# Longer DMA estimates in the plan, a second buffer for turned keys, and operands at 512-byte starts, in a planned attention and feed-forward kernel on one Trainium2 core

## The chip, the core and the metric

The kernel runs on one core of a Trainium2 chip. Its engines are TensorE (PE in the rows; PEld is its weight load), VectorE (DVE), ScalarE (ACT), GpSimd (POOL) and SyncE (SP, which issues nearly all DMAs). The metric is device time in microseconds (us) of one execution; the median of three runs is given before the change. The profile is one more execution of the same program.

## What is computed

```python
for t in range(S):                                   # attention with a decaying state
    state = alpha[:, :, t, :, None] * state + einsum('bhd,bhe->bhde', k[:, :, t], v[:, :, t])
    y[:, :, t] = einsum('bhd,bhde->bhe', q[:, :, t], state)
x = y.transpose(0, 2, 1, 3).reshape(3072, 384)
x = ((x @ w_a) * (x @ w_b)) @ w_out                  # first layer, width 1536
h = x @ w_in                                         # second layer, width 2048
out = (maximum(h, 0) + alpha2 * minimum(h, 0)) @ w_out2
```

There are 4 batches, 8 heads, 768 steps and a head size of 48, all in float32. The first layer's weights come as float64.

## The kernel before

**Tiles and stages.** The 3,072 tokens are 24 chunks of 128 steps. Four chunks make a block of 512 tokens, so there are 6 blocks, numbered 0 to 5. The attention is done chunk by chunk and leaves each block as a tile `x` (a high and a low part in fp32r, which together hold the float32 value). The first layer takes `x` block by block in units of 256 columns of weights, and the second layer does the same once all its weights are rounded and stored in DRAM.

**Products.** Every product of the two layers is three products of parts: high by high, low by high, high by low. That is `mm3` (lines 926, 927 and 929): nine matmuls of 128 by 128 by 512 for one tile in PSUM. The intermediate value is split by ACT into `gh` and by DVE into `gl` (lines 950 and 954); `a_sb` (line 1057) is the product of the two branches of the first layer. The stationary operand of a matmul is a weight tile, the moving one is `x`, `gh` or `gl`.

**Attention of a chunk.** `ra` holds the decays and `kq` the keys and queries, both loaded by SP into two buffers each. DVE makes running products with two scans: `scan_r` (line 584) runs backwards with the constant `ones`, `recip` (line 590) puts reciprocals into the constant `invs`, `scan_a` (line 594) runs forwards with `invs`, and `mul` (line 599) scales `kq` with both. From block 2 on the keys are turned by DMA and not by PE: DVE transposes 32 by 32 squares into `kt` (line 660), four DMAs take them to DRAM (line 664, `ktd`) and four bring them back as `ks` (line 674). `kt` and `ks` share one buffer, so the transposition of a chunk waits until PE has used the `ks` of the chunk before it. PE then works in two steps: `pe_cross`, and `pe_own` (lines 786 and 793), which needs the half-way state that DVE adds up (`mid`, line 813) and which also computes the scores of the next chunk (line 625), so that it needs the next chunk's scaled `kq` too.

**The order.** Nothing is scheduled by the hardware's readiness alone: a planner in the kernel (class `Graph`) places every operation on its engine by a guessed duration, a guessed latency and a key (the time at which it is wanted), then tries 1,500 random changes of the keys of operations that begin in the first 120 us, and keeps the plan whose last PE operation ends first. Each engine then runs its instructions in that fixed order. A DMA has a duration on SP and a latency after it. Where the plan leaves PE idle at the start, `fill` puts matmuls without a use there (line 342).

**Memory.** Tiles lie in SBUF in the order of their pools: const, wpool (weights), pers (`ones`, `invs`, the states `Z`, `As`), xpool (`x`), cpool, gpool (`gh`, `gl`), tp (the attention's inputs). By the sizes, the weights begin at byte 2,752 of each partition, which is 192 past a multiple of 512; `x` begins at 136,960, `gh` at 186,112 and `gl` at 192,256, each 256 past a multiple of 512. All tiles of a kind have sizes that are multiples of 512 there, so every slice that a full-size matmul reads begins at the same distance.

Of the kernel before, what the change touches and what calls it, by code (L numbers as in the profile page):

```python
# [14 lines left out]
F32 = mybir.dt.float32  # L15
# [23 lines left out]
SPLIT = ((0, 0), (1, 0))  # L39
BY_BLOCKS = 2  # L40

ON_PE = (("a", 0), ("b", 0), ("o", 0))
# [11 lines left out]
SOON = 120000  # L54
SEED, TRIES, WORLDS = 2, 1500, 2

# [12 lines left out]
class Graph:  # L69
# [11 lines left out]
    def add(self, eng, dur, fn, key, deps=(), lat=0, after=(), pool=None, burst=False, line=None):  # L81
        o = Op()
        o.pool, o.hold, o.burst = pool, [], burst
        o.eng, o.dur, o.fn, o.key, o.lat = eng, dur - LEAD.get(eng, 0), fn, key, lat + LEAD.get(eng, 0)
        o.users, o.soft, o.n = [], [], len(self.ops)
        for d in {x.n: x for x in deps if x is not None}.values():
            d.users.append(o)
        for d in {x.n: x for x in after if x is not None}.values():
            d.soft.append(o)
        if line:  # L90
            if line in self.last and self.last[line] not in [x for x in after if x is not None]:
                self.last[line].soft.append(o)
            self.last[line] = o
        self.ops.append(o)
        return o
# [203 lines left out]
def body(tc, akq, v, vg, w_a, w_b, w_o1, w_in, w_o2, beta, out):  # L299
# [13 lines left out]
    with ExitStack() as ctx:  # L313
        ctx.enter_context(tc.manual_schedule())
        pool = lambda name, bufs=1, **k: ctx.enter_context(tc.tile_pool(name=name, bufs=bufs, **k))
        const, wpool, pers = pool("const"), pool("wpool"), pool("pers")
        xpool, cpool, gpool, tp = pool("xpool", 2), pool("cpool", 2), pool("gpool", 2), pool("tp", 2)
        dram = pool("dram", space=DRAM)
# [8 lines left out]
        betaT = const.tile([P, F2], F32, name="betaT")  # L327
        ones = pers.tile([P, NJ, CH + 1], F32, name="ones")
        invs = pers.tile([P, NJ, CH + 1], F32, name="invs")
        Z = pers.tile([P, BC, NJ, D], F32, name="Z")  # L330
        At = pers.tile([P, 2 * NC], F32, name="As")
        x2d = [dram.tile([P, 2, KT, MB], F32, name=f"x2d{n}") for n in range(NB)]
# [3 lines left out]

        warm = ones.bitcast(BF16)[:, 0, 2 : 2 + 2 * CH]

# [4 lines left out]

        nc.gpsimd.memset(ones, 0.0)
        nc.gpsimd.memset(ones[:, :, 0:1], 1.0)
        nc.gpsimd.memset(invs, 0.0)
        make_identity(nc, eye)
# [174 lines left out]
        xring, lring, rring, vring = Ring(2), Ring(2), Ring(2), Ring(2)  # L522
        aring, kring, sring = Ring(1), Ring(1), Ring(1)
        both = ps_att.tile([P, 2, 2 * NC // 2], F32, name="both")
# [4 lines left out]
        state = [[] for _ in range(BC)]  # L529
        sums = [At[:, NC + i * NJ * D : NC + (i + 1) * NJ * D].rearrange("p (j d) -> p j d", d=D) for i in range(2)]  # L530
        slots = [Z[:, c] for c in range(BC)] + sums[1:]

        def place(g):
            n, c = divmod(g, BC)
            key = c * 1000 - 100000 if n == 0 else block_at[n] - (BC - c) * 12000 - 14000
            if n == 1:
# [7 lines left out]
        def inputs(g):  # L544
# [38 lines left out]
            def scan_r():  # L583
                nc.vector.tensor_tensor_scan(
                    out=s["ra"][:, 0 : NA - 1][:, ::-1], data0=s["ra"][:, : NA - 1 : -1],
                    data1=ones.rearrange("p j t -> p (j t)"), initial=0.0, op0=ALU.mult, op1=ALU.add,
                )

            def recip():
                nc.vector.reciprocal(invs[:, :, 0:1], r0())  # L590

            def scan_a():
                a = s["ra"][:, NA - 1 : 2 * NA - 2]
                nc.vector.tensor_tensor_scan(out=a, data0=a, data1=invs.rearrange("p j t -> p (j t)"),
                                             initial=0.0, op0=ALU.mult, op1=ALU.add)
# [4 lines left out]

            turned = n >= BY_BLOCKS
            r = A("DVE", 1220, scan_r, [la])
            rc = A("DVE", 180, recip, [r, before["scan"]])
            sa = before["scan"] = A("DVE", 1220, scan_a, [rc])
            slack = SLACK if not start else 0
# [35 lines left out]
        def chunk(g):  # L641
# [16 lines left out]
            def turn():  # L658
                s["kt"] = tp.tile([P, NJ, P], F32, name="kt", tag="ks", bufs=1)
                nc.vector.transpose(s["kt"], kT())  # L660

            def away(b):
                def f():
                    nc.sync.dma_start(
                        ktd[g].rearrange("t j a f -> t (j a) f")[:, :, b * SQ : (b + 1) * SQ],
                        s["kt"][b * SQ : (b + 1) * SQ].rearrange("p j (a d) -> p (j a) d", d=SQ),
                    )
# [9 lines left out]
            if turned:  # L677
                x = A("DVE", 650, turn, [k1, *kring.take()])
                lhold.append(x)
                moved = [A("SP", 430, away(b), [x], 0, 2000) for b in range(BT)]  # L680
                x = None
                back_at = []
                for a in range(BT):
                    x = A("SP", 350, back(a), moved, 0, 3800, after=[x])
                    back_at.append(x)
# [564 lines left out]
```

## Time and profile before

| | |
|---|---|
| median of 3 runs | 943.03 us (941.46 to 948.37) |
| the profiled execution | 943.25 us |
| its span, first to last instruction | 941.5 us |
| PE busy | 932.5 us, 99% of the span |
| DVE busy | 564.0 us, 60% |
| ACT busy | 245.2 us, 26% |

The page of the profile gives the busy time of each engine, the same in 40 slices of the span, and the chain of waits. Other views used below are the table by stretches of time (busy time and granted clock in each), the instructions in order of time, the groups by line and shape, and the list of waits by engine. The busy time of a matmul in the rows is from its start to its modelled end, so matmuls that follow each other overlap there; the time that one costs is the distance between starts.

### The profile page before, as it was taken

The numbers are of one execution on the slowest core, as the hardware profiler recorded it, in microseconds if no ns is written. First come the engines' busy times: TensorE is split into PE (matmuls) and PEld (weight loads), VectorE is DVE, ScalarE is ACT, GpSimd is POOL, SyncE is SP. The second block draws the span as 40 slices with busy tenths as digits, with TensorE's granted clock in tenths as the row PEclk, the third lists the DMA queues.
The fourth block names the chain that finished last, engine by engine and source line by source line (L and its number), as shares of the span: only waits on it lengthen the run. The fifth ranks groups of instructions, "written<-read, shape, count | busy, mean of one in ns | idle before, by whom it ended". The sixth has DMA issues, their size and how long they took to land.

```text
span 941.5 us, 15646 instructions
## 1 busy us (share of the span) xinstructions
PE 932.5 (99%) x6637; PEld 760.1 (81%) x6637; DVE 564.0 (60%) x865; ACT 245.2 (26%) x406; POOL 2.2 (0%) x11
## 2 busy tenths in 40 slices
PE   9999999999999999999999999999999999999998
PEld 7788887888888788787888888888888888888886
DVE  8999964674886687663232264554545545545554
ACT  3555531223333333331122121111111111111111
POOL 0000000000000000000000000000000000000000
PEclk9999999999999999999999999999999999999999
DMA  9973103563657767763266620100200200200000
GB/s 353 403 262 102 32 1 79 159 189 137 210 162 228 249 207 217 241 175 93 82 235 202 212 91 1 68 34 1 89 12 1 101 1 0 101 1 1 34 0 34
DMA packets 75238, 112.89 MB, mean 120 GB/s; under 512 B 38689, under 2 KB 48417, under 8 KB 75169
## 3 DMA queue, kind: packets, MB, share of 16 engines
q1 hardware_dynamic: 75024, 111.77, 36.1%
q8 instruction: 52, 0.85, 0.4%
q14 instruction: 18, 0.14, 0.0%
q10 hardware_dynamic: 144, 0.13, 0.0%
HBM read 78.97 MB, written 30.93 MB: 117 GB/s over the span
## 4 chain that ended last, share of the span: by engine, by line
PE 90%; DVE 5%; DMA 2%; issue 1%; SPq 1%; ACT 0%; DVEq 0%; ACTq 0%
PE acc L926 12%; PE acc L929 12%; PE acc L927 12%; PE pi L926 7%; PE pi L927 7%; PE pi L929 7%; PE pb L926 5%; PE pa L926 5%; PE pb L927 5%; PE pa L929 5%; PE pa L927 5%; PE pb L929 5%; PE both L786 2%; PE both L625 1%; DMA v<-in_v 1%; DMA ra<-in_akq 1%
## 5 line engine op out<-in xcount | busy, mean ns | idle before, releaser
L950 ACT CAST gh<-ng 128x512 fp32r<-128x512 f32 x96 | 59.5, 620 | 329.8 <-DVE ng L1163 274.0
L1159 DVE TENSOR_SCALAR ng<-pi,betaT 128x512 f32<-128x512 f32 x96 | 72.1, 751 | 105.6 <-PE pi L929 104.7
L954 DVE TENSOR_TENSOR gl<-ng,gh 128x512 fp32r<-128x512 f32 x96 | 66.3, 690 | 79.6 <-ACT gh L950 79.6
L926 PE MATMUL pi<-x,v 128*128 128x512 f32 x288 | 113.3, 393 | 0.0
L929 PE MATMUL acc<-gl,v 128*128 128x512 f32 x288 | 113.1, 393 | 0.0
L926 PE MATMUL acc<-gh,v 128*128 128x512 f32 x288 | 112.9, 392 | 0.0
L927 PE MATMUL pi<-x,v 128*128 128x512 f32 x288 | 112.7, 391 | 0.0
L927 PE MATMUL acc<-gh,v 128*128 128x512 f32 x288 | 112.1, 389 | 0.0
L1057 DVE TENSOR_TENSOR a_sb<-a_sb,pb 128x512 f32<-128x512 f32 (+1 forms) x76 | 49.9, 656 | 83.3 <-PE pb L929 83.3
L926 PE MATMUL pb<-x,wb 128*128 128x512 f32 (+1 forms) x228 | 87.8, 388 | 0.6 <-DVE a_sb L1057 0.6
L926 PE MATMUL acc<-gh,wo 128*128 128x512 f32 (+1 forms) x228 | 88.4, 388 | 0.0
L926 PE MATMUL pa<-x,wa 128*128 128x512 f32 (+1 forms) x228 | 87.3, 386 | 0.0
L929 PE MATMUL acc<-gl,wo 128*128 128x512 f32 (+1 forms) x228 | 86.8, 381 | 0.0
L927 PE MATMUL pb<-x,wb 128*128 128x512 f32 (+1 forms) x228 | 86.0, 380 | 0.5 <-DVE wb L453 0.5
L927 PE MATMUL acc<-gh,wo 128*128 128x512 f32 (+1 forms) x228 | 86.4, 379 | 0.0
L927 PE MATMUL pa<-x,wa 128*128 128x512 f32 (+1 forms) x228 | 85.9, 380 | 0.0
L950 ACT CAST gh<-a_sb 128x512 fp32r<-128x512 f32 (+1 forms) x76 | 45.3, 596 | 140.8 <-DVE a_sb L1057 131.5
L929 PE MATMUL pi<-x,v 128*128 128x512 f32 x288 | 81.6, 391 | 0.0
L1054 ACT COPY a_sb<-pa 128x512 f32<-128x512 f32 (+1 forms) x76 | 42.7, 562 | 107.1 <-PE pa L929 106.9
L1163 DVE SCALAR_TENSOR_TENSOR ng<-pi,ng 128x512 f32<-128x512 f32 x96 | 66.3, 691 | 3.1
L926 PEld LDWEIGHTS pi<-x,v 128*128 128x128 f32 x288 | 54.1, 188 | 13.7 <-DVE ng L1163 2.1
L954 DVE TENSOR_TENSOR gl<-a_sb,gh 128x512 fp32r<-128x512 f32 (+1 forms) x76 | 50.1, 659 | 25.0 <-ACT gh L950 24.9
(126 smaller groups left out, 1360.3 us busy)
## 6 DMA issues: line engine op xcount, KB each, us to landing
kq<-in_akq SPq DMA_DIRECT2D x24, 512.0 KB, 5.1
w2d<-ws SPq DMA_DIRECT2D x16, 768.0 KB, 5.1
v<-w2d SPq DMA_DIRECT2D x16, 768.0 KB, 5.9
x2d<-x SPq DMA_DIRECT2D x18, 512.0 KB, 3.7
x<-x2d SPq DMA_DIRECT2D x6, 1536.0 KB, 6.9
ra<-in_akq SPq DMA_DIRECT2D x24, 258.5 KB, 3.9
v<-in_v SPq DMA_DIRECT2D x24, 256.0 KB, 5.0
rs<-in_w_in SPq DMA_DIRECT2D x8, 768.0 KB, 6.0
```

What stands on the lines that cost most here:

```text
L625: nc.tensor.matmul(a[hs, i, j, :], kT()[ps, j, hs], qT()[ps, j, hs], start=True, stop=True, skip_group_check=True)
L786: nc.tensor.matmul(y_of(k, half(p), part_of(h)), s["v"][part_of(h), 2 * j + i, :], s["As"][part_of(h), i, j, :], start=first, stop=False, ...
L926: nc.tensor.matmul(o, lh, rh, start=first and n == 0, stop=False)
L927: nc.tensor.matmul(o, ll, rh, start=False, stop=False)
L929: nc.tensor.matmul(o, lh, rl, start=False, stop=last and n == len(pairs) - 1)
L950: nc.scalar.copy(gq[idx][0], src())
L954: nc.vector.tensor_tensor(out=gl, in0=src(), in1=gh.bitcast(F32), op=ALU.subtract)
L1054: nc.scalar.copy(b["a"], ba["t"])
L1057: nc.vector.tensor_tensor(out=b["a"], in0=b["a"], in1=bb["t"], op=ALU.mult)
L1159: nc.vector.tensor_scalar(out=b["n"], in0=bh["t"], scalar1=0.0, scalar2=betaT[:, i : i + 1], op0=ALU.min, op1=ALU.mult)
L1163: nc.vector.scalar_tensor_tensor(out=b["n"], in0=bh["t"], scalar=0.0, in1=b["n"], op0=ALU.max, op1=ALU.add)
```

## The change

The plan's figures for DMAs grow: the four DMAs that take a turned chunk away count 640 ns on SP and 3,500 ns after it (430 and 2,000 before), the four that bring it back 640 and 5,000 (350 and 3,800). Every DMA of SP that is wanted later than 110 us in the plan counts 3,500 ns more (`SPARE`). The keys of blocks 2 to 5 are spaced 16,000 ns apart instead of 12,000 (`PACE`). The seed of the random search is another one. The turned keys `kt` get a place of their own at the end of `At`, apart from `ks`. The constants `ones` and `invs` become one tile `heads`: `recip` overwrites its four first columns, and GpSimd sets them to 1.0 again after `scan_a`, before the next `scan_r` may run. Last, a pad of 320 bytes stands ahead of the weights and `pers` moves to the end, so that the weights begin at byte 3,072, `x` at 125,952, `gh` at 175,104 and `gl` at 181,248, all multiples of 512.

```diff
+PACE = 16000
+STEADY, SPARE = 110000, 3500
+PAD = 80
-SEED, TRIES, WORLDS = 2, 1500, 2
+SEED, TRIES, WORLDS = 6, 1500, 2
+        lat += SPARE if eng == "SP" and key > STEADY else 0
-        const, wpool, pers = pool("const"), pool("wpool"), pool("pers")
-        xpool, cpool, gpool, tp = pool("xpool", 2), pool("cpool", 2), pool("gpool", 2), pool("tp", 2)
+        const, wpool, xpool = pool("const"), pool("wpool"), pool("xpool", 2)
+        cpool, gpool, tp, pers = pool("cpool", 2), pool("gpool", 2), pool("tp", 2), pool("pers")
-        ones = pers.tile([P, NJ, CH + 1], F32, name="ones")
-        invs = pers.tile([P, NJ, CH + 1], F32, name="invs")
+        const.tile([P, PAD], F32, name="pad")
-        At = pers.tile([P, 2 * NC], F32, name="As")
+        At = pers.tile([P, NC + 2 * NJ * D + NC], F32, name="As")
+        heads = pers.tile([P, NJ, CH + 1], F32, name="heads")
+        kt = At[:, NC + 2 * NJ * D :].rearrange("p (j t) -> p j t", j=NJ)
-            key = c * 1000 - 100000 if n == 0 else block_at[n] - (BC - c) * 12000 - 14000
+            key = c * 1000 - 100000 if n == 0 else block_at[n] - (BC - c) * PACE - 14000
+            def begin():
+                nc.gpsimd.memset(heads[:, :, 0:1], 1.0)
-            r = A("DVE", 1220, scan_r, [la])
-            rc = A("DVE", 180, recip, [r, before["scan"]])
-            sa = before["scan"] = A("DVE", 1220, scan_a, [rc])
+            r = A("DVE", 1220, scan_r, [la, before["scan"]])
+            rc = A("DVE", 180, recip, [r])
+            sa = A("DVE", 1220, scan_a, [rc])
+            before["scan"] = A("POOL", 110, begin, [sa])
-                x = A("DVE", 650, turn, [k1, *kring.take()])
-                moved = [A("SP", 430, away(b), [x], 0, 2000) for b in range(BT)]
+                x = A("DVE", 700, turn, [k1, *tring.take()])
+                moved = [A("SP", 640, away(b), [x], 0, 3500) for b in range(BT)]
+                tring.use(*moved)
-                    x = A("SP", 350, back(a), moved, 0, 3800, after=[x])
+                    x = A("SP", 640, back(a), [*moved, *held], 0, 5000, after=[x])
```

The order changes on all engines; three places are shown. The first is SP near the end of the attention, at the last two chunks (22 and 23). `ktd` and `ks` are the way of turned keys out and back, `kq` and `v` the loads for the chunk after, `w2d`, `rs` weights of the second layer. Before:

```order
L664 DMA ktd22_142<-kt_4689 512x1x32 x4
L674 DMA ks_4754<-ktd22_142 32x4x128 x4
L565 DMA kq_4774<-in_akq 128x1024
L569 DMA v_4778<-in_v 128x512
L1084 DMA w2d15_119<-ws1_4711 128x1536
L664 DMA ktd23_143<-kt_4831 512x1x32 x4
L674 DMA ks_4894<-ktd23_143 32x4x128 x4
```

Changed:

```order
L671 DMA ktd22_142<-As_96 512x1x32 x4
L1092 DMA w2d12_116<-ws0_4608 128x1536
L569 DMA kq_4703<-in_akq 128x1024
L573 DMA v_4715<-in_v 128x512
L392 DMA rs1_4717<-in_w_o2 128x768
L681 DMA ks_4741<-ktd22_142 32x4x128 x4
L392 DMA rs0_4760<-in_w_in 128x768
L671 DMA ktd23_143<-As_96 512x1x32 x4
```

The last chunk's `kq` stood behind the four `ks` DMAs, which wait for `ktd` to land; it now stands ahead of them.

The second place is the same one on DVE: the scaling of the last chunk's `kq` and, behind it, `mid` (`As<-both,Z`), for which PE waits. Before:

```order
L732 TENSOR_TENSOR As_97<-both_155,mask_92 128x512
L880 TENSOR_TENSOR x_4606<-both_155,x_4606 128x4x128
L954 TENSOR_TENSOR gl_4759<-a_sb_4708,gh_4758 128x512
L599 TENSOR_TENSOR kq_4774<-kq_4774,ra_4328 128x1024
L1057 TENSOR_TENSOR a_sb_4802<-a_sb_4802,pb_4792 128x512
L660 STREAM_TRANSPOSE kt_4831<-kq_4774 128x512
L813 TENSOR_TENSOR As_97<-both_155,Z_96 128x192
```

Changed, up to the second row ahead of the same `mid` (line 821 there; one row of line 437 stands between):

```order
L606 TENSOR_TENSOR kq_4703<-kq_4703,ra_4326 128x1024
L667 STREAM_TRANSPOSE As_96<-kq_4703 128x512
L1065 TENSOR_TENSOR a_sb_4773<-a_sb_4773,pb_4763 128x512
L417 TENSOR_SCALAR c1_4787<-c1_4787 128x768
L962 TENSOR_TENSOR gl_4793<-a_sb_4773,gh_4792 128x512
L437 TENSOR_SCALAR rs1_4717<-rs1_4717 128x768
L441 SCALAR_TENSOR_TENSOR c2_4788<-rs1_4717 128x768
L453 TENSOR_SCALAR c1_4787<-c1_4787 128x768
L1065 TENSOR_TENSOR a_sb_4820<-a_sb_4820,pb_4810 128x512
L456 SCALAR_TENSOR_TENSOR ws1_4822<-c2_4788,c1_4787 128x768
L417 TENSOR_SCALAR c1_4834<-c1_4834 128x768
L962 TENSOR_TENSOR gl_4840<-a_sb_4820,gh_4839 128x512
```

Two rows stood between the scaling and `mid`; now there are twelve, two pairs of `a_sb` and `gl` among them.

The third place is the start of the program on DVE: scans, reciprocals and scalings of the first chunks. Before:

```order
L584 SCALAR_TENSOR_TENSOR ra_156<-ra_156,ones_94 128x516
L590 RECIPROCAL invs_95<-ra_156 128x4
L584 SCALAR_TENSOR_TENSOR ra_158<-ra_158,ones_94 128x516
L594 SCALAR_TENSOR_TENSOR ra_156<-ra_156,invs_95 128x516
L590 RECIPROCAL invs_95<-ra_158 128x4
L599 TENSOR_TENSOR kq_160<-kq_160,ra_156 128x1024
```

Changed:

```order
L588 SCALAR_TENSOR_TENSOR ra_155<-ra_155,heads_97 128x516
L594 RECIPROCAL heads_97<-ra_155 128x4
L601 SCALAR_TENSOR_TENSOR ra_155<-ra_155,heads_97 128x516
L606 TENSOR_TENSOR kq_157<-kq_157,ra_155 128x1024
L588 SCALAR_TENSOR_TENSOR ra_159<-ra_159,heads_97 128x516
L594 RECIPROCAL heads_97<-ra_159 128x4
```

The second chunk's `scan_r` stood ahead of the first chunk's `scan_a`, and now stands behind it and behind the first scaling.

## Rows read from the trace of the kernel before

**Rows 1.** The page: span, and part 1, busy us, share of the span, instructions.

```profile
span 941.5 us, 15646 instructions
...
PE 932.5 (99%) x6637; PEld 760.1 (81%) x6637; DVE 564.0 (60%) x865; ACT 245.2 (26%) x406; POOL 2.2 (0%) x11
```

**Rows 2.** The page, part 2: busy tenths and granted clock in 40 slices.

```profile
PE   9999999999999999999999999999999999999998
...
PEclk9999999999999999999999999999999999999999
```

**Rows 3.** Busy time by stretch; granted clock behind POOL, then DMA share and GB/s.

```profile
core 0: us, PE busy (x) PEld busy (x) DVE busy (x) ACT busy (x) POOL busy (x), PEclk, DMA share, GB/s
14.00:60.00 46.00, 44.82 (x627) 37.08 (x624) 45.50 (x84) 24.04 (x51) 0.00 (x0) 1.00 0.94 365
60.00:120.00 60.00, 60.00 (x579) 50.58 (x578) 60.00 (x101) 31.17 (x49) 0.00 (x0) 1.00 0.31 97
480.00:941.50 461.50, 457.91 (x1995) 373.89 (x1993) 222.70 (x319) 78.41 (x130) 0.00 (x0) 1.00 0.16 56
```

**Rows 4.** PE in order of time: start us, us, engine, line; second layer.

```profile
685.64 0.39 PE L926 MATMUL acc<-gh,v 128*128 128x512 f32 x1
...
689.76 0.39 PE L926 MATMUL acc<-gh,v 128*128 128x512 f32 x1
```

**Rows 5.** Groups of PE by line and shape: count, busy us, mean ns, idle.

```profile
L926 PE MATMUL pi<-x,v 128*128 128x512 f32 x288 | 113.3, 393 | 0.0
...
L926 PE MATMUL acc<-gh,wo 128*128 128x512 f32 x204 | 81.5, 400 | 0.0
...
L926 PE MATMUL acc<-gh,wo 128*128 128x256 f32 x24 | 6.9, 288 | 0.0
```

**Rows 6.** PE in order of time: the first unit, 256 columns wide.

```profile
23.04 0.28 PE L927 MATMUL pa<-x,wa 128*128 128x256 f32 x1
...
23.63 0.51 PE L929 MATMUL pa<-x,wa 128*128 128x256 f32 x3
```

**Rows 7.** Fill matmuls: durations (min/median/max ns), from the tile view.

```profile
L342 PE MATMUL wp<-ones x79: 270/272/421, 1.4 to 24.2; 128*128 128x256 bf16 x79
```

**Rows 8.** PE in 3.00 us of nothing but fill: busy (matmuls), clock.

```profile
6.50:9.50 3.00, 3.00 (x30) 1.00 1.01 393
```

**Rows 9.** Waits of PE: us in total, times, longest us.

```profile
PE both L786 <- DVE As L813: 2.0, 1, 2.0
...
PE pb L926 <- DVE a_sb L1057: 0.6, 1, 0.6
PE pb L927 <- DVE wb L453: 0.5, 1, 0.5
```

**Rows 10.** All engines in order of time around the longest PE wait.

```profile
422.54 0.59 SPq L565 DMA_DIRECT2D kq<-in_akq  x1
...
427.51 1.22 DVE L599 TENSOR_TENSOR kq<-kq,ra 128x1024 f32<-128x1024 f32 x1 [4.30 <-DMA kq<-in_akq]
...
429.25 0.70 DVE L660 STREAM_TRANSPOSE kt<-kq 128x512 f32<-128x512 f32 x1
...
429.88 0.32 DVE L813 TENSOR_TENSOR As<-both,Z 128x192 f32<-128x192 f32 x1
...
430.25 0.46 PE L786 MATMUL both<-As,v 64*64 64x64 f32 x16 [2.03 <-DVE As L813]
```

**Rows 11.** The same around the second wait.

```profile
380.33 1.23 DVE L584 TENSOR_TENSOR_SCAN ra<-ra,ones 128x516 f32<-128x516 f32 x1 [4.15 <-DMA ra<-in_akq]
...
384.59 0.50 PE L926 MATMUL pb<-x,wb 128*128 128x512 f32 x1 [0.64 <-DVE a_sb L1057]
```

**Rows 12.** Waits of DVE for loads: us in total, times, longest us.

```profile
DVE kq L599 <- DMA kq<-in_akq: 27.4, 10, 5.4
...
DVE ra L584 <- DMA ra<-in_akq: 10.4, 5, 4.2
```

**Rows 13.** GpSimd in order of time: the small memset of the constant.

```profile
1.38 0.10 POOL L345 MEMSET ones<- 128x4 f32 x1
```

More of the change, by code (lines that the diff above doesn't have):

```diff
@@ L334, in body @@
         ktd = [dram.tile([SQ, NJ, BT, P], F32, name=f"ktd{g}") for g in range(NG)]
-        warm = ones.bitcast(BF16)[:, 0, 2 : 2 + 2 * CH]
+        warm = heads.bitcast(BF16)[:, 0, 2 : 2 + 2 * CH]
         def fill(t0, t1):
@@ L342, in fill @@
                 nc.tensor.matmul(wp, warm[:, 0:P], warm, start=True, stop=True)
-        nc.gpsimd.memset(ones, 0.0)
-        nc.gpsimd.memset(ones[:, :, 0:1], 1.0)
-        nc.gpsimd.memset(invs, 0.0)
+        nc.gpsimd.memset(heads, 0.0)
+        nc.gpsimd.memset(heads[:, :, 0:1], 1.0)
         make_identity(nc, eye)
@@ L522, in body @@
         xring, lring, rring, vring = Ring(2), Ring(2), Ring(2), Ring(2)
-        aring, kring, sring = Ring(1), Ring(1), Ring(1)
+        aring, kring, sring, tring = Ring(1), Ring(1), Ring(1), Ring(1)
         both = ps_att.tile([P, 2, 2 * NC // 2], F32, name="both")
@@ L585, in scan_r @@
                     out=s["ra"][:, 0 : NA - 1][:, ::-1], data0=s["ra"][:, : NA - 1 : -1],
-                    data1=ones.rearrange("p j t -> p (j t)"), initial=0.0, op0=ALU.mult, op1=ALU.add,
+                    data1=heads.rearrange("p j t -> p (j t)"), initial=0.0, op0=ALU.mult, op1=ALU.add,
                 )
             def recip():
-                nc.vector.reciprocal(invs[:, :, 0:1], r0())
+                nc.vector.reciprocal(heads[:, :, 0:1], r0())
+            def begin():
+                nc.gpsimd.memset(heads[:, :, 0:1], 1.0)
             def scan_a():
                 a = s["ra"][:, NA - 1 : 2 * NA - 2]
-                nc.vector.tensor_tensor_scan(out=a, data0=a, data1=invs.rearrange("p j t -> p (j t)"),
+                nc.vector.tensor_tensor_scan(out=a, data0=a, data1=heads.rearrange("p j t -> p (j t)"),
                                              initial=0.0, op0=ALU.mult, op1=ALU.add)
@@ L658, in turn @@
             def turn():
-                s["kt"] = tp.tile([P, NJ, P], F32, name="kt", tag="ks", bufs=1)
-                nc.vector.transpose(s["kt"], kT())
+                nc.vector.transpose(kt, kT())
             def away(b):
@@ L665, in f @@
                         ktd[g].rearrange("t j a f -> t (j a) f")[:, :, b * SQ : (b + 1) * SQ],
-                        s["kt"][b * SQ : (b + 1) * SQ].rearrange("p j (a d) -> p (j a) d", d=SQ),
+                        kt[b * SQ : (b + 1) * SQ].rearrange("p j (a d) -> p (j a) d", d=SQ),
                     )
@@ L677, in chunk @@
             if turned:
-                x = A("DVE", 650, turn, [k1, *kring.take()])
+                x = A("DVE", 700, turn, [k1, *tring.take()])
                 lhold.append(x)
-                moved = [A("SP", 430, away(b), [x], 0, 2000) for b in range(BT)]
-                x = None
+                moved = [A("SP", 640, away(b), [x], 0, 3500) for b in range(BT)]
+                tring.use(*moved)
+                held, x = kring.take(), None
                 back_at = []
                 for a in range(BT):
-                    x = A("SP", 350, back(a), moved, 0, 3800, after=[x])
+                    x = A("SP", 640, back(a), [*moved, *held], 0, 5000, after=[x])
                     back_at.append(x)
```

## The prediction

> **What bounds the kernel now.** I read the page first. PE is busy for 932.5 of 941.5 us [rows 1], in every slice but the last at 90% or more, with the full clock granted throughout [rows 2]. The table by stretches asks whether another engine hides behind that. DVE is busy 45.50 of 46.00 us from 14 to 60 us and all of the 60 us after that; from 480 us to the end, where the second layer runs, PE has 457.91 of 461.50 us by itself [rows 3]. So there are three limits: DVE feeds PE up to about 120 us, PE alone sets the pace from there on, and nothing but the time of a matmul counts in the last 460 us.
>
> The price of a matmul comes next. Nineteen neighbours of the second layer start between 685.64 and 689.76 us, 18 distances in 4.12 us, so a full-size matmul costs 229 ns (the 390 ns in the rows overlap) [rows 4]. There are six groups like the first of rows 5 and nine like the second, 6 x 288 + 9 x 204 = 3,564 matmuls of 512 columns, and nine like the third, 216 of 256 columns [rows 5]. 3,564 x 0.229 = 816 us: 87% of the time is this one number.
>
> Last, the waits of PE. There are three of weight: 2.0 us for `mid`, 0.6 us for an `a_sb`, 0.5 us for a weight [rows 9]. Everything that a better order alone can give back is there or in the first 60 us.
>
> **Longer DMA estimates, spacing and the second buffer.** The longest wait can be followed row by row. The last `kq` is issued at 422.54 us, and DVE gets it at 427.51, after 4.30 us of standing still; behind it in DVE's fixed order are the transposition (429.25) and `mid` (429.88), and PE begins `pe_own` at 430.25, 2.03 us late [rows 10]. The plan gave this load 1.4 us on SP and 3.0 us after it; it took 4.97 us from issue to use. The second wait is of the same kind: DVE stood 4.15 us for an `ra`, the products behind it came late, and PE lost 0.64 us before `pb` [rows 11]. DVE stood 27.4 us in ten waits for `kq` and 10.4 us in five for `ra` [rows 12], and only these two reached PE visibly. With 3.5 us added to each such load, the load can take what it took here without arriving after its place in the plan. The order bears it out at that place: the last `kq` is issued ahead of the four `ks` DMAs, and twelve instead of two rows of DVE stand between it and `mid`. The second buffer works the same way: a transposition no longer waits for PE's use of the chunk before. By the order, the rows of DVE between a chunk's transposition and its `mid` are 7 to 70 before and 21 to 47 now, so the tight places go. I take both waits as removed: -2.0 - 0.6 = **-2.6 us**. But the scalings of `kq` are not all early now: at seven of fifteen chunks no more than three rows stand between the scaling of the next `kq` and `mid`, as many as before, at other chunks. One late load there costs what rows 10 show. I give back a third of the gain for that, **+0.9 us** (ends: 0 and 2.6). What is late next is then nothing planned; PE runs at its pace.
>
> The SP queue has a new wait too: the four `ks` DMAs wait for PE's use of the last `ks`, and loads stand behind them. Their cover is the same added 3.5 us; without it, a load that is 5 us late costs 2 us, as in rows 10, so the ends above hold it.
>
> **One constant for both scans.** The reciprocals now overwrite `heads`, and GpSimd's memset of four columns stands between a `scan_a` and the next `scan_r`, 24 times. Such a memset takes 0.10 us [rows 13]. By the order DVE always has other work between the two scans, the least being one `As` and one `Z`, or the scaling of 1.2 us [rows 10], so it is hidden; queued behind a waiting scan would be all of DVE. If the cover were gone in the eight chunks before 120 us, where DVE has no idle time [rows 3], the price would be the memset and the two signals around it, some 0.4 us by the distance between `mid` at 429.88 (0.32 us long) and PE's start at 430.25 for one signal: 8 x 0.2 to 8 x 0.4 = 1.6 to 3.2 us. I take 0.
>
> **The start.** The same 865 instructions stand on DVE. Summed by the durations in the trace, the first 14 `a_sb` and `gl` come at places between 2.5 us earlier and 3.7 us later than before, and PE's order is moved with them. The number of fills goes from 79 [rows 7] to 76 in the order, worth 3 x 0.109 = **-0.3 us**. The weight behind the 0.5 us wait comes 1.7 us earlier, others later; I take 0, with ends of -1.5 and +2.
>
> **Operands at multiples of 512.** This is the part that can be large, because it touches every matmul. What the trace shows of the price: the 30 fills that touch 3.00 us, each 0.272 us long [rows 7, 8], start within 3.27 us, 109 ns apart. At 2.4 GHz, the level that a granted clock of 1.00 stands for, 256 columns are 106.7 ns: 2.3 ns are left over. The first unit's fp32r matmuls of 256 columns are 5 distances in 0.59 us, 118 ns [rows 6], 11.3 ns over. Those of 512 columns are 229 ns, 15.6 ns over 213.3. So fp32r costs 9.0 and 13.3 ns more than the fill, and what it is that costs this no row tells: weights at 192 and moving operands at 256 past a multiple of 512 are the same for all of them. The fill speaks against the start address as the cause: its moving operand begins 196 past a multiple of 512 and runs 512 bytes, across a boundary, at 2.3 ns in all. But it is bf16. I take **0 us**. The end below is that all of the difference goes: 3,564 x 13.3 + 216 x 9.0 = 49.3 us. Nearest to a row in between: the excess grows by 4.3 ns for 256 more columns, which are 1,024 bytes, 2.15 ns for each 512. An operand that begins in the middle of such a stretch touches one stretch more than one at its start, so the saving is one in each matmul: 3,780 x 2.15 = 8.1 us. The end above is the same amount with the other sign.
>
> The Trainium skill, SBUF — State Buffer, Specifications, gives the memory's line as 16 bytes. All starts, before and after, are multiples of 16, so by that page the shift changes nothing; the trace has one placement only and can't show it. By the row's bound the sum would be 8.1 us less, by the page it is the sum below.
>
> **The sum.** 943.25 (the profiled execution, 1.75 us over its span and 0.2 over the median of 943.03) - 2.6 + 0.9 - 0.3 = 941.25, say **941 us**.
>
> **The rivals.**
> First, a stretch saved in each matmul: 941 - 8.1 = 933 us (929 to 935). For it: cost that grows with the bytes read. Against it: the fill. Chance 0.20, of which two thirds lie below 933.6.
> Second, all of the excess is placement: 941 - 49.3 = 892 us. For it: both sizes of fp32r pay and the fill does not. Against it: fp32r differs from the fill in its weights too, which are twice as wide. Chance 0.08. The Trainium skill, TensorE: Matmul & The Clock Gate, "Wait — 56ns, not 53.3ns?", has a warm matmul at its columns over 2.4 GHz plus about 2.5 ns, 215.7 ns at 512 columns. Rows 4 differ from it by 13 ns; if the page held for aligned fp32r, this rival would be the outcome.
> Third, the plan does not do what it says: the waits move to other loads, since ten already exist and the seed is new. 943 to 946 us; within 1%. Chance 0.12.
> Fourth, on the other side: weights and moving operand, 64 bytes apart in their stretches before, now start alike, and if their reads meet once in a matmul it costs. At 2.15 ns that is 941 + 8.1 = 949 us; it is slower by over 1% (952.5) from 3.0 ns on, a distance of 232 ns. For it there is no row, against it that PE's rows show one distance at any load of the other engines [rows 3, 4]. Chance 0.08, most of it short of the line.
>
> **The numbers.** The forecast has 0.52; its own range is 938 to 943. 1% is about what a measurement of this kernel tells from no change: faster means under 933.6, slower over 952.5. Faster: two thirds of 0.20, and 0.08: 0.22. Slower: half of the fourth and a little for a plan gone wrong at the start, 0.06. Within 1%: 0.72. The range must hold 0.8: forecast, third and first to 929 us make 0.84 less edges; upwards it takes in the third. 929 to 947.
>
> **What would show it.** The distance of full-size matmuls in the second layer decides the largest part: 229 ns again (forecast), 226 to 227 (first rival), about 216 (second), over 229 (fourth). The list of PE's waits should hold nothing over 1 us behind `mid` or an `a_sb`; DVE's waits for `kq` should shrink from 27.4 us. Second layer, 480 us to the end: if its length is the same to 1 us while the total moved, the plan moved it; if it moved by more, the matmuls did. The prediction is wrong if the total moves by more than 4 us with an unchanged distance, for then DVE's start or a load that I did not see sets the end.

## The result and the profile after

| | before | after |
|---|---|---|
| median beside each other, 4 runs each | 942.25 us | 934.14 us (933.29 to 934.51) |
| the profiled execution | 943.25 us | 933.95 us |
| its span | 941.5 us | 932.2 us |

The ratio is 0.9909, with an interval from 0.9888 to 0.9929: faster by 0.9%. The forecast was 941, with 929 to 947 as its range.

The page of the profile after, span and part 1 (busy us, share, instructions), answers to [rows 1].

```profile
span 932.2 us, 15662 instructions
...
PE 925.9 (99%) x6634; PEld 760.0 (82%) x6634; DVE 564.8 (61%) x865; ACT 246.2 (26%) x406; POOL 4.6 (0%) x34
```

PE is still busy for 99%, so the 9.3 us must have come out of PE's own work and its few waits. PE in order of time in the second layer, as [rows 4]:

```profile
685.40 0.39 PE L934 MATMUL acc<-gh,v 128*128 128x512 f32 x1
...
689.48 0.39 PE L934 MATMUL acc<-gh,v 128*128 128x512 f32 x1
```

Again 18 distances lie between the two, now in 4.08 us: 226.7 ns, where it was 229. Over the unbroken runs of 286 such distances in the second layer the means are 228.89 to 228.93 ns before and 226.83 after, 2.07 ns less. The table by stretches shows the same, from 600 to 800 us, before and then after (columns as in [rows 3]):

```profile
600.00:800.00 200.00, 200.00 (x872) 163.22 (x871) 104.02 (x148) 32.68 (x54) 0.00 (x0) 1.00 0.10 36
```

```profile
600.00:800.00 200.00, 199.99 (x880) 164.58 (x879) 104.43 (x150) 33.38 (x55) 0.00 (x0) 1.00 0.10 37
```

880 matmuls stand where 872 did, with the clock granted in full in both. The two longest of PE's waits (us in total, times, longest us), where [rows 9] had 2.0, 0.6 and 0.5 us:

```profile
PE wp L346 <- POOL heads L348: 1.4, 1, 1.4
PE kps L639 <- PE dS L766: 0.7, 1, 0.7
```

The first is the start of the program, which before has too, and the second is at 18.6 us. All three waits of before are gone. DVE's waits for loads, 27.4 and 10.4 us in [rows 12], are now one each:

```profile
DVE ra L588 <- DMA ra<-in_akq: 3.6, 1, 3.6
DVE kq L606 <- DMA kq<-in_akq: 1.4, 1, 1.4
```

And the place of [rows 10], all engines in order of time, the last `kq`:

```profile
407.48 0.38 SPq L569 DMA_DIRECT2D kq<-in_akq  x1
...
416.06 1.22 DVE L606 TENSOR_TENSOR kq<-kq,ra 128x1024 f32<-128x1024 f32 x1
...
429.26 0.35 DVE L821 TENSOR_TENSOR As<-both,Z 128x192 f32<-128x192 f32 x1
...
433.33 0.46 PE L794 MATMUL both<-As,v 64*64 64x64 f32 x16
```

The load is used 8.58 us after its issue, without a wait; the scaling ends 12 us ahead of `mid`, and PE takes `mid` 4 us after it begins.

So two things happened: the waits went, and every full-size matmul became 2.07 ns shorter. By the first `pi` matmul of the second layer (536.78 us before, 530.78 after) and the last matmul (937.51 and 928.21) the second layer is 400.73 and 397.43 us long. Its 6 x 288 = 1,728 matmuls of 512 columns at 2.07 ns are 3.6 us, and 3.3 came out.

### The profile page after: what moved, and what is told of

Same layout as the page of the kernel before. It is cut to its first block, busy times and chain, and to the rows that moved or that the text cites. A ratio compares the mean times of both kernels' runs of the same rounds, so it can differ in the third digit from the quotient of the medians.

```text
span 932.2 us, 15662 instructions
## 1 busy us (share of the span) xinstructions
PE 925.9 (99%) x6634; PEld 760.0 (82%) x6634; DVE 564.8 (61%) x865; ACT 246.2 (26%) x406; POOL 4.6 (0%) x34
## 4 chain that ended last, share of the span: by engine, by line
PE 96%; DVE 3%; issue 0%; ACT 0%; POOL 0%; ACTq 0%; POOLq 0%
PE acc L934 13%; PE acc L935 12%; PE acc L937 12%; PE pi L934 7%; PE pi L935 7%; PE pi L937 7%; PE pa L934 5%; PE pb L934 5%; PE pa L935 5%; PE pb L935 5%; PE pa L937 5%; PE pb L937 5%; PE both L794 2%; PE both L633 1%; PE wp L346 1%; PE both L816 1%
## 5 line engine op out<-in xcount | busy, mean ns | idle before, releaser
L934 PEld LDWEIGHTS pi<-x,v 128*128 128x128 f32 x288 | 54.1, 188 | 13.7 <-DVE ng L1171 2.6
L937 PEld LDWEIGHTS pi<-x,v 128*128 128x128 f32 x288 | 54.1, 188 | 11.3
```

The source lines that it names most:

```text
L934: nc.tensor.matmul(o, lh, rh, start=first and n == 0, stop=False)
L937: nc.tensor.matmul(o, lh, rl, start=False, stop=last and n == len(pairs) - 1)
```

## The experiments

Three theories stood at first. **S**, the prediction's first rival: each stretch of 512 bytes that an operand touches costs. **R**: what counts is how far the weights' start lies from the moving operand's start, and not where either stands by itself. **P**: the plan, or the chip of the day, and not the starts.

### The two halves of the change apart

`undo_starts` is the changed kernel with a pad and a gap that put the operands back where they were:

```diff
-PAD = 80
+PAD, GAP = 0, 16
-        const, wpool, xpool = pool("const"), pool("wpool"), pool("xpool", 2)
+        const, wpool, gap, xpool = pool("const"), pool("wpool"), pool("gap"), pool("xpool", 2)
-        const.tile([P, PAD], F32, name="pad")
+        gap.tile([P, GAP], F32, name="gap")
```

> The changed kernel with the start addresses of before: no pad ahead of the weights (192 past a multiple of 512) and 64 bytes ahead of x (x, gh, gl 256 past). Plan, seed, constants and second buffer stay. Theory S: full-size matmuls 228.9 ns apart in the second layer, total 934.1 + 7.4 = 941.5 us (940 to 942.5). Theory P: 226.8 ns and 934 us.

Measured: 940.19 us (939.5 to 940.84), ratio 0.9975 (0.9964 to 0.9986) to 942.17 beside it, 2.0 us faster than before. The distance is 228.90 ns again. Its longest PE wait after the start is 0.7 us, and DVE's waits for loads are down as in the changed kernel:

```profile
DVE ra L588 <- DMA ra<-in_akq: 3.6, 1, 3.6
DVE kq L606 <- DMA kq<-in_akq: 1.6, 1, 1.6
```

`starts_alone` is the kernel before with the new starts only (`pers` moved behind the other pools, a pad of 320 bytes, and half the scratch for DMA descriptors, to make room).

> The kernel before with the new start addresses alone: a pad of 320 bytes ahead of the weights, the pool of constants and states moved to the end, and a smaller scratch region for descriptors (512 bytes for 1,024) so that it fits; weights, x, gh and gl then begin at multiples of 512. Plan, seed and buffers are those of before. Theory S: 226.8 ns, total 942.25 - 7.4 = 934.9 us (934 to 936), with the waits of PE at 384 and 428 us still there. Theory P: 228.9 ns and 942 us.

Measured: 937.7 us (935.7 to 939.75), ratio 0.9953 (0.9938 to 0.9969): 4.5 us faster; distance 226.73 ns. The time is 2.8 us over the 934.9 of S. The old plan still has the longer of its two waits, and here it costs more than it lasts. The list of PE's waits, and the table by stretches around the place:

```profile
PE both L787 <- DVE As L814: 2.3, 1, 2.3
```

```profile
420.00:425.70 5.70, 5.70 (x53) 4.20 (x51) 1.26 (x3) 0.00 (x0) 0.00 (x0) 1.00 0.78 223
425.70:427.98 2.28, 0.01 (x1) 0.00 (x0) 2.28 (x5) 0.88 (x2) 0.00 (x0) 1.00 0.48 199
427.98:431.60 3.62, 3.62 (x83) 3.24 (x84) 1.23 (x3) 0.80 (x2) 0.00 (x0) 0.53 0.35 59
431.60:435.00 3.40, 3.40 (x16) 2.81 (x15) 1.72 (x4) 0.62 (x1) 0.00 (x0) 1.00 0.22 51
```

PE did nothing for 2.28 us, and in the 3.62 us behind that the granted clock was 0.53, nearly all of it at the lower level of 1.2 GHz. After the wait of 2.03 us in [rows 10] it had stayed at 1.00. The stretch of lower clock is worth some 1.7 us by an estimate from these rows (3.62 us at 0.53 of the clock), and so part of the miss; 7.4 us was also too much for the starts, as the part on the prediction shows. What follows: the two halves are worth 2.0 and some 4.5 to 6 us; P alone can't be all, since the distance goes with the starts and not with the plan.

### Matmuls alone, with every start

`m1_sweep` leaves out everything but matmuls: 36 in a row for each pair of starts, weights and moving operand in steps of 64 bytes.

```python
for i, (a, c, k) in enumerate(pairs * 4):
    nc.tensor.matmul(t, ws[:, a, dw + 2*k*P : dw + 2*k*P + P],
                     xs[:, c, dm + k*MB : dm + k*MB + cols], start=i == 0, stop=i == 35)
```

> A kernel of matmuls alone, which computes nothing of the reference: stretches of 36 matmuls (nine pairs of operands, four times), each stretch with other start addresses of the moving operand (ma to mh: 0, 64, ... 448 bytes past a multiple of 512) and of the weights (wa to wh, the same). Theory S, that a start inside a 512-byte stretch costs one stretch more: ma_wa has matmuls 226.8 ns apart, every other m with wa about 229, and wb to wh add nothing or the same step once, whatever the distance. Theory R, that the distance between the two operands counts: ma_wa, mb_wb, ... mh_wh are alike at 226.8 and the rest is slower. Theory P, that start addresses are nothing and the plan or the chip made the 2.1 ns: all 64 stretches within 0.3 ns. For 256 columns S expects 117.5 ns where the start is inside and 115 where it is not; for bf16 no difference by any theory, as the fill of before had 2.3 ns over its columns at a start of 196.

PE in order of time; `ma_wb` is moving operand at 0 and weights at 64 past a multiple of 512, `half_` has 256 columns, `bf_` is bf16. The cost of one matmul is the distance to the start of the next row, by 36.

```profile
30.72 8.32 PE L56 MATMUL ma_wa<-x,w 128*128 128x512 f32 x36
38.88 8.56 PE L56 MATMUL ma_wb<-x,w 128*128 128x512 f32 x36
47.27 8.53 PE L56 MATMUL ma_wc<-x,w 128*128 128x512 f32 x36
55.64 8.41 PE L56 MATMUL ma_wd<-x,w 128*128 128x512 f32 x36
63.89 8.34 PE L56 MATMUL ma_we<-x,w 128*128 128x512 f32 x36
72.07 8.56 PE L56 MATMUL ma_wf<-x,w 128*128 128x512 f32 x36
...
97.08 8.42 PE L56 MATMUL mb_wa<-x,w 128*128 128x512 f32 x36
105.34 8.33 PE L56 MATMUL mb_wb<-x,w 128*128 128x512 f32 x36
113.51 8.56 PE L56 MATMUL mb_wc<-x,w 128*128 128x512 f32 x36
...
561.78 4.47 PE L56 MATMUL half_ma_wa<-x,w 128*128 128x256 f32 x36
566.09 4.41 PE L56 MATMUL half_mb_wa<-x,w 128*128 128x256 f32 x36
570.34 4.43 PE L56 MATMUL half_mc_wa<-x,w 128*128 128x256 f32 x36
574.61 4.25 PE L56 MATMUL half_md_wa<-x,w 128*128 128x256 f32 x36
578.70 4.46 PE L56 MATMUL half_me_wa<-x,w 128*128 128x256 f32 x36
...
687.51 7.93 PE L56 MATMUL bf_full_mb<-lo,lw 128*128 128x512 bf16 x36
695.28 7.93 PE L56 MATMUL bf_full_mc<-lo,lw 128*128 128x512 bf16 x36
```

With the moving operand at 0 the weights at 0, 64, 128, 192 give 8.16, 8.39, 8.37, 8.25 us for 36: 226.7, 233.1, 232.5 and 229.2 ns; at 256 it is 8.18 us, 227.2, as at 0. With the moving operand at 64 the whole row moves by one: `mb_wa` 229.4, `mb_wb` 226.9. The first few matmuls of a row can differ from the rest; then the distances repeat. In all 64 pairs, which are in steps of 64 bytes, the time goes with one number, weights' start less moving start, modulo 256 bytes (bf16 has its weights at 0 throughout and moves only the other operand):

| weights less moving, modulo 256 | 0 | 64 | 128 | 192 |
|---|---|---|---|---|
| fp32r, 512 columns, ns | 226.7 to 227.9 | 233.3 to 233.4 | 232.1 to 232.4 | 229.1 to 229.2 |
| fp32r, 256 columns, ns | 119.4 to 119.7 | 113.7 to 114.3 | 118.5 to 118.6 | 117.9 |
| bf16, 512 / 256 columns, ns | 215.8 to 216.1 / 109.2 | 215.8 / 109.2 | 215.8 / 109.2 | 215.8 / 109.2 |

One row of 16 with 256 columns falls out (weights 192, moving 0: 113.4 here, 117.8 in the next sweep, each held over its 36 matmuls), so for 256 columns the starts alone don't fix the time; why is open. A last row repeats 0 against 0 and comes to 229.6 over all, with 320 ns behind its first matmul; from the fifth distance on it has 226.7 again. The kernel before had 192 and 256, a difference of 192; the changed one has 0. That is R with both its numbers, 229.1 and 226.7. S falls: both operands at 64 cross a boundary each, and cost the least.

`m2_fine` is the same kernel with steps of 4 bytes for the weights, and of 16 for 256 columns:

> Leaves out everything but matmuls: 36 matmuls a row, weights moved in steps of 4 bytes from 0 to 252 past a multiple of 512 against moving operands that stay at 0 (512 columns), then in steps of 16 bytes for 256 columns with the moving operand at 0 and at 64. R (the distance from the moving operand's start to the weights' start, modulo 256 bytes, sets the time): the rows at 0, 64, 128 and 192 give again 226.7 to 227.3, 233.4, 232.4 and 229.1 ns; with 256 columns the row for weights at 64 + d and moving at 64 equals the row for weights at d and moving at 0, to 0.3 ns. If 0 is the best there is, no row lies under 226.6 ns at 512 columns. S (each stretch of 512 bytes that an operand touches costs): all rows but the first are alike, about 2 ns over it. P (the plan or the chip of the day): all rows alike, about 229 or about 227.

PE in order of time; `wja`, `wjb` and `wjc` are weights at 144, 148 and 152 against 0 with 512 columns; `half_a_e` is weights at 64 and moving at 0, `half_e_i` weights at 128 and moving at 64.

```profile
332.44 8.33 PE L52 MATMUL wja<-x,w 128*128 128x512 f32 x36
340.61 8.57 PE L52 MATMUL wjb<-x,w 128*128 128x512 f32 x36
349.01 8.49 PE L52 MATMUL wjc<-x,w 128*128 128x512 f32 x36
...
583.08 4.25 PE L52 MATMUL half_a_e<-x,w 128*128 128x256 f32 x36
587.17 4.44 PE L52 MATMUL half_a_f<-x,w 128*128 128x256 f32 x36
...
668.10 4.26 PE L52 MATMUL half_e_i<-x,w 128*128 128x256 f32 x36
672.19 4.44 PE L52 MATMUL half_e_j<-x,w 128*128 128x256 f32 x36
```

Measured: no step lies under 226.66 ns. Six of 64 (0, 120, 144, 156, 204, 252) come to between 226.66 and 226.77, most others to 230 to 233.5, and the worst, 164, to 237.3; 144 (`wja`: 8.17 us by 36) and 148 (8.40) are neighbours. All 16 rows of 256 columns with the moving operand at 64 repeat those at 0 to 0.32 ns, moved by 64. The difference of 0 that the change made is as good as any for 512 columns.

In these steps of 4 bytes only the weights move. `m1_sweep` also has the moving operand at 4, 16 and 32 bytes with the weights at 0, which are differences of 252, 240 and 224. Its row for 4 with the next one, and then the row of `m2_fine` with the same difference and the moving operand at 0 (`wpd`, weights at 252), also with the next one:

```profile
629.27 8.72 PE L56 MATMUL fine_mfour<-x,w 128*128 128x512 f32 x36
637.83 8.50 PE L56 MATMUL fine_msixteen<-x,w 128*128 128x512 f32 x36
```

```profile
557.84 8.33 PE L52 MATMUL wpd<-x,w 128*128 128x512 f32 x36
566.01 4.48 PE L52 MATMUL half_a_a<-x,w 128*128 128x256 f32 x36
```

The moving operand at 4 costs 237.7 ns, where `wpd` has 226.7; at 16 it costs 231.4, where the weights at 240 have 228.3; at 32 the two agree (233.2 and 233.1). So R is shown for starts in steps of 64 bytes, as all starts of the kernel are, and refuted in finer steps: there the moving operand's own start counts too.

For 256 columns the difference of 0 is a poor one: 113.3 ns is to be had at 64 in the sweep, against 119.4 in the changed kernel. In the whole kernel less of it is seen: `apart_64`, below, has that difference, and its matmuls of 256 columns that follow each other stand 116.6 ns apart, 216 x 2.8 ns = 0.6 us under the changed kernel's.

### The same in the whole kernel

Three versions of the changed kernel shift only the gaps between pools, with the same order of instructions.

```diff
 weights_only: weights at 0, x, gh, gl at 256 past a multiple of 512
+PAD, GAP = 80, 64
 moving_only: weights at 192, x, gh, gl at 0
+PAD, GAP = 0, 80
 apart_64: weights at 0, x, gh, gl at 192
+PAD, GAP = 80, 48
```

> The changed kernel with x, gh and gl where they were (256 past a multiple of 512) and only the weights at 0. R: the distance from moving operand to weights is 0 modulo 256 as in the changed kernel, so 226.8 ns a matmul and 933.5 to 935 us. S: weights touch one stretch less, moving operands one more, as much as before if the moving ones count: 229 ns and about 940 us; if only the weights count, 226.8 ns. P: 934 by the plan alone.

> The changed kernel with the weights where they were (192 past a multiple of 512) and only x, gh and gl at 0. R: the distance is 192 modulo 256 as before the change, so 228.9 ns a matmul and 939.5 to 941 us, as with both starts undone (940.2). S: one stretch less for the moving operands, 226.8 ns and 934 us, if they count; 229 ns if only weights count. P: 934 by the plan alone.

> The changed kernel with the weights at 0 and x, gh and gl at 192 past a multiple of 512, so that the weights start 64 bytes further, modulo 256. R: 233.4 ns a matmul of 512 columns and 113.7 ns instead of 119.4 for one of 256: 934.1 + 3564 x 0.0066 - 216 x 0.0057 = 956 us, slower than the kernel before by 1.5%. S: at most the time of the kernel before, 229 ns and 940 us. P: 934.

| | difference modulo 256 | us | distance, ns | ratio to before |
|---|---|---|---|---|
| weights_only | 0 | 933.95 (933.72 to 935.17) | 226.78 | 0.9911 (0.9891 to 0.9930) |
| moving_only | 192 | 940.11 (939.71 to 941.32) | 228.90 | 0.9976 (0.9967 to 0.9986) |
| apart_64 | 64 | 954.16 (954.05 to 954.84) | 233.32 | 1.0124 (1.0101 to 1.0147) |

The table by stretches of `apart_64`, 600 to 800 us, answers to the two rows of the result: 857 matmuls, where 872 and 880 stood.

```profile
600.00:800.00 200.00, 200.00 (x857) 160.28 (x856) 101.77 (x145) 32.08 (x53) 0.00 (x0) 1.00 0.10 36
```

All three came out as R said, `apart_64` 1.8 us under its 956 (and its 256 columns at 116.6 ns, not at 113.7). `weights_only` puts the moving operands off their boundary and loses nothing; `moving_only` puts them on it and gains nothing. So multiples of 512 are not needed; equal starts modulo 256 do the same. The same change with the starts 64 bytes apart would have been slower than before by 1.2%.

### What removed the waits

Four more kernels take the plan apart, with the starts of the changed kernel: theory **E**, the longer estimates; **B**, the second buffer; **L**, luck with a new order. A last one tests **T**, that both belong together.

```diff
 old_costs: the old figures
-PACE = 16000
-STEADY, SPARE = 110000, 3500
+PACE = 12000
+STEADY, SPARE = 110000, 0
-                moved = [A("SP", 640, away(b), [x], 0, 3500) for b in range(BT)]
+                moved = [A("SP", 430, away(b), [x], 0, 2000) for b in range(BT)]
-                    x = A("SP", 640, back(a), [*moved, *held], 0, 5000, after=[x])
+                    x = A("SP", 350, back(a), [*moved, *held], 0, 3800, after=[x])
 one_buffer: kt and ks in one buffer
+                s["kt"] = tp.tile([P, NJ, P], F32, name="kt", tag="ks", bufs=1)
-                x = A("DVE", 700, turn, [k1, *tring.take()])
+                x = A("DVE", 700, turn, [k1, *kring.take()])
-                tring.use(*moved)
-                held, x = kring.take(), None
+                held, x = [], None
 seed_2
-SEED, TRIES, WORLDS = 6, 1500, 2
+SEED, TRIES, WORLDS = 2, 1500, 2
```

> The changed kernel with the old figures for DMAs and the old spacing (430 and 2,000, 350 and 3,800 ns, SPARE 0, PACE 12,000); the second buffer, the one constant, the new seed and the starts stay. E (the longer estimates removed the waits for late loads): the waits come back, one or more of 0.6 to 2.5 us on PE behind mid, an a_sb or a kq after 290 us, and the time is 2 to 3.5 us over the changed kernel, 936 to 938 us, near the kernel before with the new starts alone (937.7). B (the second buffer did it): no such wait, 934 us. L (any new order might have done it): anything between.

> The changed kernel with kt and ks in one buffer again, in the same place in memory as before; all estimates, the one constant, the seed and the starts are those of the changed kernel. E: 934 us to within 0.7, no wait of PE over 1 us behind mid or a_sb. B: the waits come back, 936 to 938 us.

> The changed kernel with the old seed of the random search, 2, and all else as changed. E: 934 us to within 1 (the search only moves operations that begin in the first 120 us), no wait of PE over 1 us after 120 us. L: a difference of 2 us or more from the changed kernel.

> The changed kernel itself, so that the three beside it are compared on one chip. All theories: 933.3 to 934.6 us, distance of full-size matmuls in the second layer 226.8 ns.

> The changed kernel with one buffer for kt and ks and the old figures for DMAs and old spacing together; the one constant, the new seed and the starts stay. T (the long estimates and the second buffer belong together: long estimates make the shared buffer the limit of the plan, short ones make no use of a second): 937 to 939 us, as the kernel before with the new starts alone (937.7), no wait of PE behind the x of a block over 1 us, and waits behind mid of 1 to 3 us. O (the one constant or the new seed cost or gave something by themselves): 2 us or more away from 937.7. B (the shared buffer itself is slow under the new constant): over 945 us, with waits behind the x of a block as with one buffer and long estimates (975).

| us | old figures | new figures |
|---|---|---|
| one buffer | 937.96 (both_undone) | 974.98 (one_buffer) |
| second buffer | 939.32 (old_costs) | 933.95 (same_again) |

`same_again` spans 933.35 to 934.43. `seed_2` is 934.77 (934.14 to 935.37), and its longest PE wait after the start is 0.6 us, at 37 us: the seed gives some 0.8 us at most. `old_costs` is 1.3 us over the 938 that E allowed. The intervals of the ratios to before are 0.9955 to 0.9983 for `old_costs`, 1.0320 to 1.0373 for `one_buffer`, 0.9948 to 0.9973 for `both_undone`.

The longest of PE's waits with the old figures (the `wp` row, of the start, is left out), and then with one buffer:

```profile
PE both L794 <- DVE Z L824: 2.7, 2, 1.9
...
PE cl L484 <- DVE a_sb L1065: 1.3, 1, 1.3
PE both L794 <- DVE x L888: 0.6, 1, 0.6
```

```profile
PE pa L934 <- DMA x<-x: 29.6, 7, 8.6
```

The wait of 1.9 us with the old figures, at 333 us, goes back to late weights and not to a late `kq`: ACT waited 3.99 us for an `rs` until 324.01, and DVE then had work without a pause until `mid`. With one buffer PE waits at the start of blocks for their `x`, 29.6 us in seven waits. The miss of 41 us against E (934) is not a matter of late loads. By the plan's own figures a turned chunk in a shared buffer takes 0.70 us on DVE, 4 x 0.64 + 3.5 + 3.5 out, and 4 x 0.64 + 5.0 + 3.5 back: 21.3 us before PE may use it and the next transposition may begin. Four chunks make 85 us; a block lasts (530.78 - 50.95) / 6 = 80 us. With the old figures they are 0.65 + 4 x 0.43 + 2.0 + 4 x 0.35 + 3.8 = 9.6, 38 us a block. So by the plan's figures the chain of turned keys is longer than a block, and the trace agrees: the 16 transpositions of `one_buffer` begin 20.4 us or more apart, 25.1 us on average, four 100 us, where 10 of the 15 distances of `both_undone` are 12 to 20 us. The order is fixed, so this is the plan's spacing; no run has the old spacing of the keys with the other new figures, which would part the two. The idle stretches also take the clock, as the table by stretches of `one_buffer` shows around a wait of 5.15 and one of 3.80 us:

```profile
312.00:319.00 7.00, 2.39 (x4) 1.01 (x4) 0.50 (x1) 0.00 (x0) 0.00 (x0) 0.50 0.54 128
319.00:320.50 1.50, 1.18 (x3) 1.00 (x4) 0.00 (x0) 0.00 (x0) 0.00 (x0) 0.50 1.06 410
...
321.80:330.00 8.20, 8.20 (x152) 6.86 (x152) 6.62 (x13) 3.07 (x5) 0.44 (x1) 0.91 1.03 304
```

T holds by its times: the second buffer by itself makes the kernel 1.4 us slower (within the spread of the two, 936.5 to 942.0), the new figures by themselves 37 us slower, and both together make it 4.0 us faster. B falls as a cause by itself, and E as well. T's sign in the waits did not come: `both_undone` has no wait of PE behind `mid` over 1 us, but one of 1.3 us behind an `a_sb`. The late loads follow the figures: DVE's waits for `kq` are 23.2 us in `both_undone` and 15.1 in `old_costs`, 3.7 in `one_buffer`, and none is listed in `same_again`. Which of the new figures does it (the four DMAs', `SPARE` or `PACE`) no run parts. `both_undone` is 0.3 us from `starts_alone` (937.7), so the one constant and the seed together are worth nothing that can be measured.

## Why the prediction held, and where it did not

**The bound.** Right: PE at 99%, and the time of a matmul is what is left to gain.

**The waits.** Right in place, and near in size, in part by luck. The plan was given -2.6 + 0.9 - 0.3 = -2.0 us, and `undo_starts`, which is the plan alone, is 2.0 us under before. The part of +0.9 has no visible cause, though: no load came late in its place, the waits for `kq` fell from 27.4 to 1.4 us, and by the spans of the two profiles (941.5 and 938.6) 2.9 us went. The profile of before was 1.1 us above the median of that comparison, so whether anything was given back is open. The second wait of before, 0.64 us, is also absent in `starts_alone`, which has the old plan with the new starts. I named the estimates and the buffer as two ways to the same gain; the runs show one way that needs both.

**One constant.** Right at 0. The 0.2 to 0.4 us that the prediction set for each chunk if the cover were gone read a signal too dear: 429.88 + 0.32 leaves 0.05 us to PE's start at 430.25, which makes some 0.2 us. In order of time at the start, where DVE has no idle time, the scaling covers the memset:

```profile
5.08 1.23 DVE L601 TENSOR_TENSOR_SCAN ra<-ra,heads 128x516 f32<-128x516 f32 x1
6.35 1.23 DVE L606 TENSOR_TENSOR kq<-kq,ra 128x1024 f32<-128x1024 f32 x1
6.38 0.11 POOL L597 MEMSET heads<- 128x4 f32 x1 [3.88 <-DVE ra L601]
7.50 1.23 DVE L588 TENSOR_TENSOR_SCAN ra<-ra,heads 128x516 f32<-128x516 f32 x1
```

**The start.** 76 fills, as counted. The first full-size matmul starts at 50.74 us before and 50.95 after: 0.2 us, inside -1.5 to +2.

**Operands at multiples of 512.** This is the step that failed: 0 us was taken, and it is -6.2 us (`moving_only` 940.11, `weights_only` 933.95, on one chip with one order). With the -2.0 us of the plan that makes -8.2, where 8.1 came out. By the traces of these two kernels it is made up so. The second layer is 3.65 us shorter (401.06 and 397.41). In the first layer the distances fall by 1.5 ns (`pa`, 612 matmuls), 1.6 (`pb`, 612), 0.4 (`acc` with `gh`, 408) and 4.0 (`acc` with `gl`, 204), 2.9 us together, 1.6 ns for each instead of 2.1; why it is less there is open. The 216 of 256 columns became slower, 116.7 to 119.4 ns, and take 0.6 back. That leaves 6.0. Two errors led to 0. The fill was taken as a witness against the start address; but bf16 costs 215.8 to 216.1 ns at each of the eight moving starts of the sweep, so its row could say nothing on fp32r. And I saw one placement, and looked at where each operand stands, not at the two together. The first rival (933) has the time almost exactly, and its 2.15 ns for each matmul is close to 2.07, but its mechanism is refuted: stretches of 512 don't count, and the fourth rival's side was as near, since most differences cost more than the old one did, up to 237.7 ns. So that the measured 934 lies in the range is owed to a rival whose mechanism is refuted, and is luck as far as the starts go.

The Trainium skill, SBUF — State Buffer, Specifications, gives lines of 16 bytes, from which the prediction concluded that a shift by multiples of 16 changes nothing. Here the measurement differs and decides: shifts by 64, 128 and 192 bytes moved the time of an fp32r matmul by 2.4 to 6.7 ns. The Trainium skill, TensorE: Matmul & The Clock Gate, "Wait — 56ns, not 53.3ns?", has 215.7 ns at 512 columns. The bf16 rows of the sweep agree (7.77 us by 36, 215.8); fp32r came to no less than 226.66 at any start that was tried, so the second rival (892) had no ground.

**What would show it.** The distance (226 to 227), the second layer's length (by 3.3 us, over the 1 us that was set), PE's waits and DVE's waits for `kq` answered as the prediction listed them, and they point to the first rival's number and to the plan's removal of the waits, both at once.

## What to carry to other kernels

Where fp32r matmuls make up the time, measure their distance against the difference of the two operands' starts, and place the pools so that it falls on a good one. A row of 36 matmuls for each pair of starts foretold the kernel's 512 columns to 0.2 ns (226.8, 228.9 and 233.3), but not its 256 columns. A witness of another type (bf16 here) says nothing about this. In this fixed order, longer estimates for transfers paid only where no shared buffer turned them into a chain that is longer than the loop it serves.

## What the hardware showed that was not expected

- An fp32r matmul of 128 by 128 by 512 costs 226.7 to 237.7 ns by the operands' starts, and a step of 4 bytes can be worth 7 ns (144 and 148). In steps of 64 bytes only the difference of the two starts modulo 256 counts; at 4 and 16 bytes the moving operand's own start does too. What in the chip does this is not known; that the next weights are read while the moving operand streams would fit, and no run tested it.
- For 256 columns the order of the differences is another one: 113.3 ns at 64, where 512 columns have 233.4, and 119.5 at 0, where they have the least. The same starts (192 and 0) gave 113.4 in one sweep and 117.8 in the other.
- A wait of PE can cost twice: behind 2.28 us without a matmul the granted clock was 0.53 over 3.62 us, while behind one of 2.03 us it stayed at 1.00.
